# A hand-written instruction order, laid over the whole first layer and not over its first block alone

## The chip, the cores and the metric

The kernel runs on one core of a Trainium2 chip. The metric is device time in microseconds (us) of one execution. The kernel before has a median of 888.12 us over 3 runs (887.09 to 888.78).

The core has engines with an instruction queue each: TensorE (PE, matrix products; PEld is its loading of stationary operands), VectorE (DVE), ScalarE (ACT) and SyncE (SP), which here issues the DMAs. GpSimd (POOL) does four small instructions in this kernel. Each engine takes its instructions in the order in which they stand in the program for it, so the order is decided when the kernel is built, and an instruction whose operand is late holds up what stands behind it.

## The reference

```
# 1. attention: 4 x 8 heads, 576 positions, 64 wide; window 32, half the heads with every fourth key
scores = where(mask, scale * q @ k.T, -1e9); attn = softmax(scores); x = attn @ v      # -> 2304 x 512
# 2. layer 1: 2304 tokens, 512 -> 2048 -> 512, rational activation
h = x @ w_in;  P = a0 + a1 h + a2 h^2 + a3 h^3;  Q = 1 + |b0||h| + |b1|h^2
x = (P / (Q + 1e-6)) @ w_out
# 3. layer 2: the same sizes, PReLU
h = x @ w_in;  g = max(h, 0) + alpha * min(h, 0);  out = g @ w_out
```

## The kernel before, in words

**Precision.** A float32 operand is split in a high and a low part (`xh`, `xl`; `gh`, `gl`; `wouth`, `woutl`), and a product is three matmuls: high by high, low by high, high by low. To split costs one ACT copy and one DVE subtraction (L742, L743).

**Stages.** The tokens are six blocks of 384. Attention works in units of two heads and two segments, spread over the kernel's first 400 us or so and woven into layer 1. Layer 1 goes block by block; within a block over 16 chunks of 128 of the hidden width, two at a time, which gives 48 steps `J`. A step does the input product of its two chunks (`inproj`, L645, into the PSUM banks `ps_h`), the rational activation in two parts (`rat_1`: ACT L663, L664 and DVE L665, L666, which read `ps_h`, the last of them freeing the bank; `rat_2`: DVE L672, ACT L673 and L674, DVE L675 to L677), the split of the result (L684, L685: `gh`, `gl`) and, two steps later, the output product (`outproj1`, L695, groups of three matmuls). ACT and DVE also do the softmax of the attention unit that is due (L492 to L532), the making of the packed weights of both layers (L381 to L400, `win` and `wout` tiles) and the splitting of weights (L416, L417).

**Layer 2** works on double blocks (`n` is 0 to 2) and pairs of chunks (`q` is 0 to 7), so 24 calls of `st_pair`, `k` = 0 to 23. Each does seven products (`product`, L836) in place of eight, in the order p1 p6 p2 p7 p4 p5 p3, on sums and differences of the tokens (`st_B11`, `st_T1` to `st_T4`, `st_B21`, `st_B22`; made on DVE at L760 and split at L743) and of the weights (`st_s`, `st_a`; `st_prep`, L813 and L760, split at L743). The results are put together on DVE (L866) and ACT (L871), then PReLU (`st_prelu`, L843), its split (`st_g`), and the output product (`outproj2`, L714), which is queued in the list `todo` and taken from it by `out_some(k)`. What layer 1 has left in `todo` when layer 2 begins (16 groups of three matmuls) is taken between the products of pairs 0 and 1.

The tokens that layer 2 reads go through memory: layer 1 stores them (`y_dram<-os`), and `x_load` and `y_load` (L739) load them again, into buffers that attention's loads use before. So do the packed weights: `w_dram_in` is stored (L360) and later loaded (`w` at L806, L341).

**What sets the order.** The build puts instructions on each engine by their place in the code, as far as operands and buffers allow. The kernel lays an order of its own over this: `in_order_of_need` (L136) takes the instructions built, derives who needs whom from their regions, and gives each a duration (`_cost`) and a `level`, the length of the longest chain behind it. Then it plays the program through: at each step the engine that can start earliest takes, of what is ready, the instruction with the highest level. SP stays in the order of the code, and PE's matmuls are drawn to it. What starts before `ORDERED` (115e3 ns, in the list's own time) gets a dependency on its predecessor on the engine, without a semaphore; all that starts later is only placed behind the last of these, in the build's own order. For a DMA the list counts a transfer time, and then 900 ns until its data can be used, or 2700 ns when transfers queue.

**Places that the change and the steps touch.** L136 to L262 `in_order_of_need`; `st_pair` with its four `out_some(counts[..])`; the loop over `n` and `q` at the end of the kernel; L959 to L970 the matmuls on constant data that PE does at the start (`warm`, and `fill` on `msk`).

Of the kernel before, what the change touches and what calls it, by code (L numbers as in the profile page):

```python
# [29 lines left out]
FILLS = (64,)  # L30
W_BIAS = 2.0 ** -112
NARROW = 2.1
SLACK = 100.0
FILL = 256
ORDERED = 115e3
SIGNED = (('out', 4), ('out', 6), ('out', 8), ('out', 10), ('out', 12))
WARM = 10
ORDER = "cqiqpvqvqvvwwwwwwqvwwwwwwwwqv"
# [94 lines left out]
    return i.engine == mybir.EngineType.PE and _columns(i.outs[0]) == FILL  # L133


def in_order_of_need(tc, nc, places):  # L136


    Engine = mybir.EngineType
    todo = [  # L140
        i for i in nc.cur_bb.bb.instructions
        if i.engine in (Engine.PE, Engine.DVE, Engine.Activation, Engine.SP) and (i.ins or i.outs)
    ]
    n = len(todo)
# [80 lines left out]
            waiting[todo[k].engine].append(k)  # L225
    order = {e: [] for e in free}
    landed = 0.0
    for _ in range(n):
        pick = None
        for e, w in waiting.items():  # L230
            if not w:
                continue
            t = min(max(free[e], ready_at[k]) for k in w)
            if pick is None or t < pick[0]:
                pick = t, e
        t, e = pick
        limit = max(t, free[e]) + SLACK
        k = max((k for k in waiting[e] if ready_at[k] <= limit), key=lambda k: level[k])
        waiting[e].remove(k)
        start = max(free[e], ready_at[k])  # L240
        if start < ORDERED:
            order[e].append(k)
        free[e] = start + costs[k][0]
        if e == Engine.SP:
            parts, width = size[k]
            begin = max(start + 1600, landed)
            landed = begin + parts * width / (412 if parts == 128 else 210)
            done = landed + (2700 if begin > start + 1700 else 900)
        else:
            done = start + costs[k][1]  # L250
        for j, data in after[k]:
            left[j] -= 1
            ready_at[j] = max(ready_at[j], done if data else free[e])
            if not left[j]:
                waiting[todo[j].engine].append(j)
# [11 lines left out]
def attn_rational_prelu_kernel(  # L267
# [16 lines left out]
    nc = tc.nc  # L284
# [3 lines left out]
    slots = {}  # L288
# [563 lines left out]
    def st_pair(n, q, w, counts, before):  # L852

        c = 2 * q
        after = n + 1 if q == NQ - 1 and n + 1 < SB else 0

        def free(*names):
            for name in names if after else ():
                x_place(after, name)

        def fetch(name):
            if after:
                x_fetch(after, name)

        small = n == 0 and q < 2
        add = lambda out, a, b: nc.vector.tensor_tensor(out=out, in0=a, in1=b, op=ALU.add)  # L866
        p1 = product(n, w, "A11", "B11")
        p6 = product(n, w, "S2", "T2")
        v1 = ap_.tile([128, BLK], F32, tag="pts", name="v1", bufs=2)
        u2 = ap_.tile([128, BLK], F32, tag="p", name="u2")  # L870
        nc.scalar.activation(out=v1, in_=p1, func=AF.Copy)  # L871
        add(u2, v1, p6)
        if small:
            before()
        out_some(counts[0])
        fetch("B11")

        (h0, n0, g0), (h1, n1, g1) = (
            [tp.tile([128, 2 * BLK], F32, tag=f"t{s}", name=f"t{s}", bufs=2) for s in "abc"] for _ in range(2)
        )  # L880
        p2 = product(n, w, "A12", "B21")
        p7 = product(n, w, "S3", "T3")
        add(half(h0, 0), v1, p2)
        add(half(h1, 1), u2, p7)
        out_some(counts[1])
        fetch("B21")
        free("T2")

        p4 = product(n, w, "A22", "T4")
        p5 = product(n, w, "S1", "T1")  # L890
        add(half(h1, 0), half(h1, 1), p4)
        add(half(h1, 1), half(h1, 1), p5)
        add(u2, u2, p5)
        if small:
            st_prelu(c + 1, h1, n1, g1)
            out_some(counts[2])
        free("T3", "B11")

        p3 = product(n, w, "S4", "B22")
        add(half(h0, 1), u2, p3)  # L900
        if not small:
            before()
            free("B21", "T4", "T1", "B22")
            st_prelu(c + 1, h1, n1, g1)
        hl1 = st_g(g1)
        st_prelu(c, h0, n0, g0)
        out_some(counts[3])

        def rest():
            hl0 = st_g(g0)  # L910
            for i, hl in ((1, hl1), (0, hl0)):
                for b in range(2):
                    for t in range(3):
                        todo.append((
                            outproj2, (2, 2 * n + b, c + i), [half(x, b) for x in hl], t,
                            q == 0 and i == 1, q == NQ - 1 and i == 0,
                        ))
        return rest
# [175 lines left out]
    for n in range(SB):  # L1094
        for q in range(NQ):
            k = n * NQ + q

            def before():
                if rest:
# [17 lines left out]
                    if q == (6 if n == 0 else 5):  # L1117
                        x_combine(n + 1)

            rest = st_pair(n, q, st_ops.pop(k), ((4, 4, 3, 3), (2, 0, 0, 9), (0, 0, 0, 12))[min(k, 2)], before)  # L1120
    rest()
    out_some(len(todo))
    in_order_of_need(tc, nc, slots)


def _consts():
# [79 lines left out]
```

## Time and profile before

| | |
|---|---|
| median of 3 runs | 888.12 us (887.09 to 888.78) |
| the profiled execution | 887.51 us, of which the span 885.7 us |
| PE busy | 872.5 us (99%), 5746 matmuls |
| PEld busy | 779.0 us (88%) |
| DVE busy | 760.7 us (86%), 1199 instructions |
| ACT busy | 613.3 us (69%), 1253 instructions |
| moved by DMA | 92.78 MB, mean 105 GB/s |

The span is the time from the first recorded instruction to the last; some 1.8 us of the execution lie around it. Busy times are of the whole span; matmuls are pipelined, and two that overlap count as one stretch of busy time. PE busy for 99% therefore doesn't tell how fast matmuls followed each other; their starts do. In a stretch where nothing delays them, matmuls on 384 columns start 173 ns apart.

### The profile page before, as it was taken

The page shows a single profiled execution, that of the slowest core. Times are in us where ns is not written, and L with a number is a line of the kernel's source. Part 1 is how long each engine was busy: PE and PEld are TensorE (multiplying, and loading weights), DVE is VectorE, ACT ScalarE, POOL GpSimd, SP SyncE. Part 2 cuts the span into 40 slices and gives each one's busy share as a digit, 9 for nine tenths or more (in the row PEclk, how much of TensorE's full clock was granted, in tenths as well). Part 3 has the DMA queues.
Part 4 walks back from the last instruction along what each step waited for, and adds up shares of the span by engine and source line. Part 5 has one row for each costly group of instructions (what it writes and reads, how often), then busy time and mean ns, then how long its engine had stood idle before and what let it go on. Part 6 is the DMA issues. An engine that isn't in the chain of part 4 may idle for free.

```text
span 885.7 us, 14822 instructions
## 1 busy us (share of the span) xinstructions
PE 872.5 (99%) x5746; PEld 779.0 (88%) x5746; DVE 760.7 (86%) x1199; ACT 613.3 (69%) x1253; POOL 0.2 (0%) x4
## 2 busy tenths in 40 slices
PE   9999999999999999999999999999999999999997
PEld 6555678999999999999999999898888989899896
DVE  5999999999999998988899999998986778767652
ACT  6999988788877888887677576557554456635423
POOL 0000000000000000000000000000000000000000
PEclk9999999999999999999999999999999999999999
DMA  9964212133334434440021242323320011210001
GB/s 346 407 238 176 82 57 79 38 115 140 130 109 139 173 125 148 160 149 19 20 78 42 95 131 95 119 79 119 101 85 24 27 46 60 97 47 25 1 0 72
DMA packets 32903, 92.78 MB, mean 105 GB/s; under 512 B 3905, under 2 KB 11329, under 8 KB 32833
## 3 DMA queue, kind: packets, MB, share of 16 engines
q1 hardware_dynamic: 32832, 91.83, 29.9%
q8 instruction: 45, 0.74, 0.3%
q14 instruction: 26, 0.20, 0.1%
HBM read 76.61 MB, written 15.20 MB: 104 GB/s over the span
## 4 chain that ended last, share of the span: by engine, by line
PE 57%; ACT 18%; DVE 18%; DMA 4%; issue 2%; SPq 0%; ACTq 0%
PE ps_h L836 19%; PE ps_y L714 14%; PE ps_y L695 9%; PE ps_h L645 7%; PE ps_aS L714 4%; PE ps_aP L714 3%; ACT p L512 3%; DVE tb L675 2%; DVE tc L676 2%; ACT p L532 2%; ACT tc L664 2%; ACT ta L673 2%; DVE tc L677 2%; ACT ta L674 2%; ACT ta L663 1%
## 5 line engine op out<-in xcount | busy, mean ns | idle before, releaser
L645 PE MATMUL ps_h<-xh,winh 128*128 128x384 f32 x320 | 110.4, 345 | 2.7 <-DVE tc L666 2.2
L695 PE MATMUL ps_y<-gh,wouth 128*128 128x384 f32 x320 | 108.4, 339 | 0.0
L695 PE MATMUL ps_y<-gl,wouth 128*128 128x384 f32 x320 | 107.1, 335 | 0.3 <-DVE gl L685 0.3
L695 PE MATMUL ps_y<-gh,woutl 128*128 128x384 f32 x320 | 107.2, 335 | 0.0
L645 PE MATMUL ps_h<-xh,winl 128*128 128x384 f32 x320 | 107.2, 335 | 0.0
L645 PE MATMUL ps_h<-xl,winh 128*128 128x384 f32 x320 | 107.1, 335 | 0.0
L714 PE MATMUL ps_y<-wouth,gl 128*128 128x512 f32 x192 | 74.9, 390 | 0.0
L714 PE MATMUL ps_y<-woutl,gh 128*128 128x512 f32 x192 | 74.9, 390 | 0.0
L714 PE MATMUL ps_y<-wouth,gh 128*128 128x512 f32 x192 | 74.8, 390 | 0.0
L663 ACT ACTIVATE ta<-ps_h,root 128x384 f32<-128x384 f32 x96 | 57.3, 596 | 18.7 <-PE ps_h L645 18.4
L664 ACT ACTIVATE tc<-ps_h,co 128x384 f32<-128x384 f32 x96 | 66.5, 694 | 0.0
L645 PEld LDWEIGHTS ps_h<-xh,winh 128*128 128x128 f32 x320 | 60.0, 188 | 6.9 <-DVE tc L666 3.7
L742 ACT ACTIVATE gh<-tc 128x768 fp32r<-128x768 f32 x48 | 40.3, 841 | 30.5 <-PE ps_aP L714 28.0
L695 PEld LDWEIGHTS ps_y<-gl,wouth 128*128 128x128 f32 x320 | 60.2, 188 | 0.6 <-DVE gl L685 0.6
L645 PEld LDWEIGHTS ps_h<-xl,winh 128*128 128x128 f32 x320 | 60.1, 188 | 0.3
L743 DVE TENSOR_TENSOR gl<-tc,gh 128x768 fp32r<-128x768 f32 x48 | 45.8, 954 | 16.9 <-ACT gh L742 16.7
L695 PEld LDWEIGHTS ps_y<-gh,wouth 128*128 128x128 f32 x320 | 60.2, 188 | 0.0
L742 ACT ACTIVATE st_a<-w 128x1024 fp32r<-128x1024 f32 x24 | 25.5, 1061 | 50.1 <-PE ps_h L836 41.4
L695 PEld LDWEIGHTS ps_y<-gh,woutl 128*128 128x128 f32 x320 | 60.1, 188 | 0.0
L645 PEld LDWEIGHTS ps_h<-xh,winl 128*128 128x128 f32 x320 | 60.1, 188 | 0.0
L675 DVE SCALAR_TENSOR_TENSOR tb<-tb,ta 128x768 f32<-128x768 f32 x48 | 45.8, 955 | 16.3 <-ACT ta L674 16.0
L666 DVE SCALAR_TENSOR_TENSOR tc<-tc,co,ps_h 128x384 f32<-128x384 f32 x96 | 58.1, 608 | 0.7
(197 smaller groups left out, 2317.8 us busy)
## 6 DMA issues: line engine op xcount, KB each, us to landing
w<-w_dram_in SPq DMA_DIRECT2D x24, 512.0 KB, 3.6
raw<-in_w_in_dram SPq DMA_DIRECT2D x16, 512.0 KB, 5.1
raw_inh<-in_w_out_dram SPq DMA_DIRECT2D x13, 512.0 KB, 3.8
ld_qk<-in_qk_d_dram SPq DMA_DIRECT2D x12, 512.0 KB, 5.0
ld_v<-in_v_d_dram SPq DMA_DIRECT2D x12, 512.0 KB, 4.1
ld_qk<-in_qk_p_dram SPq DMA_DIRECT2D x12, 416.0 KB, 4.2
ld_v<-in_v_p_dram SPq DMA_DIRECT2D x12, 384.0 KB, 3.4
y_dram<-os SPq DMA_DIRECT2D x24, 192.0 KB, 1.9
```

Of the source, the lines that this page charges most:

```text
L512: nc.scalar.activation(out=a["p"][h][:m, t * n:(t + 1) * n], in_=a["s"][h][:m, t * n:(t + 1) * n], func=AF.Exp, scale=scale, bias=a["nm"][ ...
L532: nc.scalar.activation(out=pv, in_=pv, func=AF.Copy, scale=rd[:m, t:t + 1])
L645: nc.tensor.matmul(out=hp[:, :BLK], lhsT=w, rhs=x, start=(k == 0), stop=(k == len(pairs) - 1))
L663: nc.scalar.activation(out=ta, in_=hp, func=AF.Abs, scale=root)
L664: nc.scalar.activation(out=tc_, in_=hp, func=AF.Identity, scale=co[:, 3:4], bias=co[:, 2:3])
L666: nc.vector.scalar_tensor_tensor(out=tc_, in0=tc_, scalar=co[:, 1:2], in1=hp, op0=ALU.add, op1=ALU.mult)
L675: nc.vector.scalar_tensor_tensor(out=tb, in0=tb, scalar=C1, in1=ta, op0=ALU.add, op1=ALU.mult)
L695: nc.tensor.matmul(out=yt[:, :BLK], lhsT=w[:, m * 128:(m + 1) * 128], rhs=g, start=(c == 0 and i == 0), stop=(c == NC - 1 and i == len(pai ...
L714: nc.tensor.matmul(out=yt, lhsT=g[:, tok], rhs=w, start=(first and i == 0), stop=(last and i == 2))
L742: nc.scalar.activation(out=hi, in_=t, func=AF.Copy)
L743: nc.vector.tensor_tensor(out=lo, in0=t, in1=hi.bitcast(F32), op=ALU.subtract)
L836: nc.tensor.matmul(out=hp, lhsT=u[:, ws], rhs=x[:, xs], start=(k == 0), stop=(k == 5))
```

## The change

1. `in_order_of_need` is given only the instructions that are built before pair `k = LISTED = 1` of layer 2, that is attention, all of layer 1 and pair 0 of layer 2 without the part called `rest`. `ORDERED` goes from 115e3 to 2000e3 ns, so all of these get an order. What is built later gets none from the list.
2. The delay between a transfer's end and its use: it was 2700 ns where transfers queue and 900 ns elsewhere. It is now `min(2700, 300 + 450 * transfers issued before)` for the first twelve and wherever they queue, so 300 ns for the first, 750 for the second, and 2700 from the seventh on.
3. The 16 groups left from layer 1 are all taken in pair 0 of layer 2, four at each of its four places (before 4, 4, 3 and 3, and two in pair 1). `out_some(counts[3])` moves ahead of the last PReLU and its split, and pairs from 1 on take 12 groups there (pair 1 took 9 before, and 2 at its first place).

```
-ORDERED = 115e3
+LAG = 2700
+LISTED = 1
+ORDERED = 2000e3
...
-def in_order_of_need(tc, nc, places):
+def in_order_of_need(tc, instructions, places):
...
-        i for i in nc.cur_bb.bb.instructions
+        i for i in instructions
...
     landed = 0.0
+    issued = []
...
-            done = landed + (2700 if begin > start + 1700 else 900)
+            done = landed + (min(LAG, 300 + 450 * len(issued)) if begin > start + 1700 or len(issued) < 12 else 900)
+            issued.append(k)
...
         if not small:
             before()
             free("B21", "T4", "T1", "B22")
+            out_some(counts[3])
             st_prelu(c + 1, h1, n1, g1)
+        else:
+            out_some(counts[3])
         hl1 = st_g(g1)
         st_prelu(c, h0, n0, g0)
-        out_some(counts[3])
...
             k = n * NQ + q
+            if k == LISTED:
+                listed = len(nc.cur_bb.bb.instructions)
...
-            rest = st_pair(n, q, st_ops.pop(k), ((4, 4, 3, 3), (2, 0, 0, 9), (0, 0, 0, 12))[min(k, 2)], before)
+            rest = st_pair(n, q, st_ops.pop(k), ((4, 4, 4, 4), (0, 0, 0, 12), (0, 0, 0, 12))[min(k, 2)], before)
     rest()
     out_some(len(todo))
-    in_order_of_need(tc, nc, slots)
+    in_order_of_need(tc, nc.cur_bb.bb.instructions[:listed], slots)
```

In the changed kernel the lines of the code in question have numbers that are higher by 4. The names below have the number of their tile behind them.

**Place 1: DVE at the start of the second block of layer 1** (around 230 to 236 us in the trace of before). `tc_2662` and `tb_2661` belong to the block's first step, `sm_2691` and `rd_2708` to the softmax of the attention unit that is due, `gl_2811` to the step before the last. Before:

```order
L685 TENSOR_TENSOR gl_2811<-tc_2512,gh_2810 128x768
L396 SCALAR_TENSOR_TENSOR win2_2983<-raw_2981,win2_2983 128x512
L522 TENSOR_SCALAR sm_2691<-sm_2691 112x8
L523 RECIPROCAL rd_2708<-sm_2691 112x8
L665 TENSOR_TENSOR tc_2662<-tc_2662,ps_h_2663 128x384
L672 SCALAR_TENSOR_TENSOR tb_2661<-ta_2660,ratio_112 128x768
L666 SCALAR_TENSOR_TENSOR tc_2662<-tc_2662,co_110,ps_h_2663 128x384
```

And after:

```order
L669 TENSOR_TENSOR tc_2662<-tc_2662,ps_h_2663 128x384
L500 TENSOR_SCALAR nm_2642<-mx_2641 112x8
L670 SCALAR_TENSOR_TENSOR tc_2662<-tc_2662,co_110,ps_h_2663 128x384
L689 TENSOR_TENSOR gl_2811<-tc_2512,gh_2810 128x768
L676 SCALAR_TENSOR_TENSOR tb_2661<-ta_2660,ratio_112 128x768
L669 TENSOR_TENSOR tc_2662<-tc_2662,ps_h_2676 128x384
L670 SCALAR_TENSOR_TENSOR tc_2662<-tc_2662,co_110,ps_h_2676 128x384
L526 TENSOR_SCALAR sm_2691<-sm_2691 112x8
L527 RECIPROCAL rd_2708<-sm_2691 112x8
```

The two readers of the bank `ps_h_2663` (L669 and L670) stand ahead of `gl_2811`, of the softmax sums and of L676; before they stood behind all of these. On ACT the instruction that they need (L664 before, L668 after) stood behind the eight exponentials of `sm_2691`, and now stands ahead of all eight.

**Place 2: DVE at the end of layer 1** (around 482 to 500 us in the trace of before). `tc_5494`, `tc_5573` and `tc_5667` are the activations of the last three steps of layer 1. Before:

```order
L676 SCALAR_TENSOR_TENSOR tc_5494<-tc_5494,co_110,ta_5492 128x768
L665 TENSOR_TENSOR tc_5573<-tc_5573,ps_h_5574 128x384
L677 SCALAR_TENSOR_TENSOR tc_5494<-tb_5493,tc_5494 128x768
L666 SCALAR_TENSOR_TENSOR tc_5573<-tc_5573,co_110,ps_h_5574 128x384
L665 TENSOR_TENSOR tc_5573<-tc_5573,ps_h_5587 128x384
L672 SCALAR_TENSOR_TENSOR tb_5572<-ta_5571,ratio_112 128x768
L666 SCALAR_TENSOR_TENSOR tc_5573<-tc_5573,co_110,ps_h_5587 128x384
L685 TENSOR_TENSOR gl_5709<-tc_5494,gh_5708 128x768
```

And after:

```order
L680 SCALAR_TENSOR_TENSOR tc_5494<-tc_5494,co_110,ta_5492 128x768
L764 TENSOR_TENSOR st_T1_5397<-st_T3_5396,st_B11l_5393 128x768
L681 SCALAR_TENSOR_TENSOR tc_5494<-tb_5493,tc_5494 128x768
L669 TENSOR_TENSOR tc_5573<-tc_5573,ps_h_5574 128x384
L764 TENSOR_TENSOR st_T3_5396<-st_B22_5399,st_T3_5396 128x768
L670 SCALAR_TENSOR_TENSOR tc_5573<-tc_5573,co_110,ps_h_5574 128x384
L764 TENSOR_TENSOR st_t2_5479<-st_B22_5399,st_T1_5397 128x768
L669 TENSOR_TENSOR tc_5573<-tc_5573,ps_h_5587 128x384
L676 SCALAR_TENSOR_TENSOR tb_5572<-ta_5571,ratio_112 128x768
L670 SCALAR_TENSOR_TENSOR tc_5573<-tc_5573,co_110,ps_h_5587 128x384
L764 TENSOR_TENSOR st_T4_5398<-st_B21l_5395,st_t2_5479 128x768
L689 TENSOR_TENSOR gl_5709<-tc_5494,gh_5708 128x768
```

`st_T1_5397` is the first of the instructions with which DVE prepares layer 2's first pair. Of these, 16 stood ahead of the first row of this piece before, and all 16 stand behind it now, woven into the rows up to p1's successor on DVE (`u2_5767`) and a few behind that.

**Place 3: SP, the loads for layer 2.** `w_dram_in14` is the store of the last packed weight tile of layer 2, `st_...` the loads of its tokens. Before:

```order
L441 DMA ld_v_4535<-in_v_d_dram 128x1024
L739 DMA st_T3_5396<-y_dram1_0_88 128x384
L739 DMA st_T3_5396<-y_dram1_1_89 128x384
L341 DMA w32_5488<-w_dram_out0_2658 128x1024
L360 DMA w_dram_in14_5244<-win14_5236 128x1024
L806 DMA w32_5490<-w_dram_in0_2278 128x1024
L739 DMA st_B11l_5393<-y_dram0_0_84 128x384
```

And after:

```order
L706 DMA y_dram4_3_103<-os_5229 128x384
L360 DMA raw_5232<-in_w2_in_dram 128x1024
L360 DMA raw_5234<-in_w2_in_dram 128x1024
L364 DMA w_dram_in14_5244<-win14_5236 128x1024
L743 DMA st_B11l_5393<-y_dram0_0_84 128x384
L743 DMA st_B11l_5393<-y_dram0_1_85 128x384
L743 DMA st_T3_5396<-y_dram1_0_88 128x384
L743 DMA st_T3_5396<-y_dram1_1_89 128x384
```

The token loads stand behind the store of `win14`, whose making on DVE ends, after the change, one row behind L680 of `tc_5410`, the step before `tc_5494`. Before, `win14` was made and stored some 90 us earlier in the trace, and only the first token load stood ahead of it.

## Rows read from the trace of the kernel before

**Rows 1.** The page: busy time of each engine, and the chain that ended last.

```profile
PE 872.5 (99%) x5746; PEld 779.0 (88%) x5746; DVE 760.7 (86%) x1199; ACT 613.3 (69%) x1253; POOL 0.2 (0%) x4
...
PE 57%; ACT 18%; DVE 18%; DMA 4%; issue 2%; SPq 0%; ACTq 0%
```

**Rows 2.** Windows: busy us and instructions by engine, clock, DMA share, GB/s.

```profile
4.40:20.00 15.60, 15.52 (x266) 12.29 (x266) 9.46 (x33) 10.57 (x62) 0.00 (x0) 1.00 1.01 392
20.00:120.00 100.00, 96.78 (x638) 60.14 (x635) 97.72 (x168) 98.92 (x227) 0.00 (x0) 1.00 0.56 210
120.00:440.00 320.00, 316.62 (x2591) 301.80 (x2590) 296.59 (x462) 257.80 (x638) 0.00 (x0) 1.00 0.33 110
440.00:484.00 44.00, 44.00 (x256) 44.00 (x255) 42.91 (x59) 31.57 (x47) 0.00 (x0) 1.00 0.16 52
484.00:520.00 36.00, 36.00 (x206) 35.56 (x205) 34.61 (x51) 23.63 (x36) 0.00 (x0) 1.00 0.32 101
520.00:640.00 120.00, 119.30 (x598) 107.33 (x597) 114.28 (x178) 72.94 (x95) 0.00 (x0) 1.00 0.31 103
```

**Rows 3.** Waits of PE from 120 to 440 us: us in total, times, longest.

```profile
PE ps_h L645 <- DVE tc L666: 2.2, 4, 0.8
PE ps_h L645 <- DVE xl L615: 0.5, 1, 0.5
PE ps_h L582 <- ACT wouth L416: 0.4, 1, 0.4
PE ps_y L695 <- DVE gl L685: 0.3, 1, 0.3
```

**Rows 4.** Timeline of PE, one such wait: start, us, [idle <- releaser].

```profile
234.19 0.34 PE L695 MATMUL ps_y<-gh,woutl 128*128 128x384 f32 x1
235.28 0.45 PE L645 MATMUL ps_h<-xh,winh 128*128 128x384 f32 x1 [0.75 <-DVE tc L666]
```

**Rows 5.** Timeline of PE at the start, alike matmuls together.

```profile
2.14 3.00 PE L963 MATMUL ps_h<-warm 128*128 128x512 bf16 x8
...
6.11 2.58 PE L967 MATMUL ps_h<-msk 128*128 128x256 bf16 x22
8.62 0.29 PE L478 MATMUL ps_aS<-ld_qk 64*64 64x96 f32 x1
```

**Rows 6.** Timeline of ACT ahead of 233 us: first and last exponentials.

```profile
230.02 0.33 ACT L512 ACTIVATE p<-ps_aS,nm 112x80 f32<-112x80 f32 x1 [0.16 <-DVE nm L496]
...
232.37 0.24 ACT L512 ACTIVATION_READ_ACCUMULATOR p<-ps_aP,nm 112x1 f32 x1
232.47 0.71 ACT L664 ACTIVATE tc<-ps_h,co 128x384 f32<-128x384 f32 x1
```

**Rows 7.** Timeline of DVE, there and at 476 and 483 us.

```profile
233.21 0.55 DVE L665 TENSOR_TENSOR tc<-tc,ps_h 128x384 f32<-128x384 f32 x1 [0.15 <-ACT tc L664]
233.68 1.02 DVE L672 SCALAR_TENSOR_TENSOR tb<-ta,ratio 128x768 f32<-128x768 f32 x1
234.61 0.61 DVE L666 SCALAR_TENSOR_TENSOR tc<-tc,co,ps_h 128x384 f32<-128x384 f32 x1
...
476.12 1.01 DVE L676 SCALAR_TENSOR_TENSOR tc<-tc,co,ta 128x768 f32<-128x768 f32 x1
...
483.44 1.01 DVE L676 SCALAR_TENSOR_TENSOR tc<-tc,co,ta 128x768 f32<-128x768 f32 x1
```

**Rows 8.** Lines of DVE from 400 to 484 us: xcount, busy us, mean ns, idle.

```profile
L417 DVE TENSOR_TENSOR woutl<-w,wouth 128x1024 fp32r<-128x1024 f32 x1 | 1.2, 1218 | 0.0
L743 DVE TENSOR_TENSOR st_a<-w,st_a 128x1024 fp32r<-128x1024 f32 x1 | 1.2, 1217 | 0.0
...
L760 DVE TENSOR_TENSOR st_T<-st_T,st_B11l 128x768 f32<-128x768 f32 x1 | 0.9, 945 | 0.0
...
L760 DVE TENSOR_TENSOR st_s<-w,st_s 128x256 f32<-128x256 f32 x1 | 0.4, 415 | 0.0
```

**Rows 9.** Timeline of PE: first matmul of p1, of p4, of pair 1's p1.

```profile
498.00 0.33 PE L836 MATMUL ps_h<-st_B11h,st_a 128*128 128x384 f32 x1
...
506.32 0.33 PE L836 MATMUL ps_h<-st_T4h,st_a 128*128 128x384 f32 x1
...
512.56 0.33 PE L836 MATMUL ps_h<-st_B11h,st_a 128*128 128x384 f32 x1
```

**Rows 10.** Timeline of SP's queue from 383 to 403 us.

```profile
383.07 0.79 SPq L739 DMA_DIRECT2D st_T<-y_dram  x2
...
389.13 0.49 SPq L360 DMA_DIRECT2D w_dram_in<-win  x1
...
402.82 0.80 SPq L739 DMA_DIRECT2D st_B<-y_dram  x2
```

**Rows 11.** DMA issues from 380 to 405 us: KB each, us to landing.

```profile
w<-w_dram_in SPq DMA_DIRECT2D x1, 512.0 KB, 5.5
st_T<-y_dram SPq DMA_DIRECT2D x2, 192.0 KB, 3.2
...
st_B<-y_dram SPq DMA_DIRECT2D x2, 192.0 KB, 3.5
```

## The prediction

> **What bounds the kernel now.** I read the page's busy line and the chain first [rows 1], then the windows by stage, which say more. From 20 to 120 us ACT and DVE are busy for 98.92 and 97.72 of 100 us and PE's loads for only 60.14: attention and the making of weights bound that stage. From 120 us on it is PE: 316.62 of 320 us to 440, then all of 44, all of 36, and 119.30 of 120 [rows 2]. But DVE stands close behind: 42.91 of 44, 34.61 of 36, 114.28 of 120. So from 120 us there are two questions only: how much of PE's idle time goes, and whether DVE, which has 1.1 us to spare from 440 to 484 and 1.4 us from 484 to 520, can take work that comes later than it did.
>
> The waits of PE from 120 to 440 us add up to 2.2 + 0.5 + 0.4 + 0.3 = 3.4 us in seven places [rows 3]. One of the four on DVE's L666, of up to 0.8 us, shows in the timeline [rows 4]: the last matmul of the old block starts at 234.19, the first of the new at 235.28, where one step is 0.17; the interval lost is therefore 0.92 us, and 0.75 of it is idle.
>
> **The first 115 us.** The list ordered these before too. What changes in them comes from the smaller landing delays and the other levels. Along DVE and ACT the same instructions change places by one or two; the work ahead of any of them moves by about 1 us and back, and nothing leaves this stage. PE gets three of its ten warm matmuls and ten of its 22 fillers (the 22 take 2.58 us [rows 5]) moved behind products of attention; these products begin when their data lands (8.62 us in rows 5), so the fillers were no work that anything waited for. I take 0, with 1.5 us to either side: the moved fillers and warm matmuls take 10 x 2.58 / 22 + 3 x 3.00 / 8 = 2.3 us [rows 5], and more than half of that would have to fall on the path.
>
> By the Trainium skill, "TensorE: Matmul & The Clock Gate", section "Part 1: The HAM clock gate", TensorE's clock comes up with activity and falls without it, so fillers taken away could leave the first products at 1.2 GHz; the rows show a granted clock of 1.00, which is 2.4 GHz, from 4.4 us on [rows 2], with the fillers in place, and cannot show the other case. It would cost at most the start's own products twice, inside the 1.5 us.
>
> **Layer 1 from 120 to 440 us: the gain.** Why PE waited at 235: ACT does eight exponentials from 230.02 on, and reaches L664 at 232.47 [rows 6]; then DVE does L665, L672 (1.02 us) and L666, which frees the bank at 234.61 + 0.61 = 235.22 [rows 7]; PE goes on at 235.28. After the change (place 1) L664's successor stands ahead of all eight exponentials, 2.4 us sooner, and DVE has both readers of the bank ahead of the step's 1.02 us. Either alone covers 0.92 us. The same pattern stands at the starts of the next blocks, with alike moves: that is L666's 2.2 us. The other three waits (0.5, 0.4, 0.3) are single ones, each with its releaser further ahead after the change. The gain is 3.4 us by idle time; by the starts of the matmuls it is 4.7 us over the seven, as 0.92 stands for 0.75 at 235 us, since each new start adds some 0.2 us. I take 4.0. It can't be more than 4.7: elsewhere in the stage PE waits for nothing. It is less where the list, which knows costs only, makes waits of its own; so 2 to 4.7.
>
> **The end of layer 1: the loss.** DVE's preparation for layer 2's first pair stood spread between 406 and 482 us, ahead of L676 of `tc_5494` (483.44 us [rows 7]). In the changed order sixteen of these instructions stand behind that row (place 2). They are ten on 768 columns, of which one stands in rows 8 (0.95 us each), two on 1024 (1.22 each) and four on 256 (0.42 each) [rows 8]: 10 x 0.95 + 2 x 1.22 + 4 x 0.42 = 13.6 us. On DVE an instruction follows the one before some 0.08 us before that one's recorded end (233.68 + 1.02 to 234.61 in rows 7), so they occupy 12.3 us. What would they have instead? Ahead of 484 DVE has 12 us less to do and nothing to do it for: PE is full from 440 to 484 [rows 2], so layer 1's steps come no sooner, and DVE just waits. Behind 484 it has 34.61 + 12.3 = 46.9 us of work in a stretch of 36. Some other preparation (two splits of 768 and part of pair 1's) moves still further behind, which leaves 11.6 us ahead of the first PReLU of pair 0.
>
> How much of that reaches PE? Following both engines down the new order, from 484 on, with durations from these rows: each DVE instruction starts when the one before it is through and its operands are there, and each product starts when its bank is free and its split tokens and weights are there.
> - p1 needs the low part of `st_a`: it comes 2.3 us later than 498.00 [rows 9].
> - p6 needs the bank that the last L670 of layer 1 frees, behind twelve of the sixteen: 4.1 us late. p2 and p7 follow at about 4.
> - p4 (506.32 [rows 9]) needs a bank that DVE's L870 frees behind the split of T4: 6.1; p5 and p3 6.2 and 6.4.
> - p1 of pair 1 (512.56 [rows 9]): 6.8; its p6 and p7 7.1 and 7.6; the first output products, which need `gl` of pair 0, 7.6.
>
> The delay grows while DVE's backlog of 11.6 us lasts, less the slack that each product had against its bank or `gl` (by the trace's starts and ends 0.3 to 4 us). From about 530 us on DVE, with 120 - 114.28 = 5.7 us to spare up to 640 [rows 2], falls behind no further, and PE has the delay and keeps it, because it has no idle time to give back. I take 8 us, from 6 (the slacks larger than I count, or the output products of layer 1, now sixteen groups in this pair, filling part of the wait) to 10 (the tail of the backlog delays pair 1's products once more).
>
> **Loads.** `win14` is made later now, and the token loads stand behind its store on SP (place 3). In the trace of before they were issued at 383 to 403 us [rows 10]; now not before DVE is through with the last row of `win14`, right behind L680 of `tc_5410`; that step is 7 us ahead of `tc_5494` (476.12 against 483.44 in rows 7), so about 477.5 us. The first four loads, which `st_T1` needs, go out by 479.5 at 0.4 us each [rows 10] and land 3.2 to 3.5 us later [rows 11], at 483, when DVE comes to it; behind it on DVE stand the activations of layer 1's last two steps, for which PE would have to wait. I take 0, with 4 us more if loads land later.
>
> **Layer 2 behind that and the end.** PE's two waits at 623 to 625 us (the rest of 120 - 119.30 [rows 2]) may go or stay: 0, to 0.7 either way. All of layer 1's output groups in pair 0, and 12 in place of 9 + 2 in pair 1, move PE work earlier and shorten the list of output products left at the end by three groups; their matmuls are done all the same, so the sum is 0.
>
> **Sum.** 887.5 - 4.0 + 8 + 0 = 891.5 us against the profiled execution of 887.51, whose span of 885.7 has 1.8 us around it. It lies 0.6 us below the median of 888.12, which I let stand: forecast 891.5, 3.4 us above the median. A difference under 0.2% (1.8 us) can't be told from no change here.
>
> **Rivals.**
> - *Only PE's gaps count.* The waits of layer 1 go and the preparation, though late, finds DVE free: DVE gets ahead before 484 after all, or the list put it as late as it is needed and no later. Then 887.5 - 4.0 + 0 to 1.5 = 883.5 to 885. For it: the list knows how long DVE is busy, and puts the chain of layer 2 by its length. Against it: 46.9 us do not fit in 36. Chance 0.22. This is what the Trainium skill, "Perfetto Trace Analysis", section "Optimization Strategy", would have one do: find the gaps on the engine that bounds the stage and what it waits for. It doesn't count the second engine, which has no gaps there either [rows 2].
> - *Both cancel.* The delay of p1 to p4 is half of what I work out, because sixteen groups of layer 1 (48 x 0.173 = 8.3 us of matmuls) cover it: 887.5 - 4 + 4 = 887.5. Chance 0.2.
> - *Loads late, one place more.* The store of `win14` holds the loads on SP, 8 token loads and then three loads of 512 KB land after DVE asks for them, and DVE stands at `st_T1` in front of layer 1's last two activations: on top of 891.5 come the 3.2 to 5.5 us that such a load takes [rows 11], so 894.7 to 897. For it: SP now is in the order of the code up to there. It decides if the store is issued after 480 us. Chance 0.13.
> - *The change does nothing beyond 115 us*, the order being held by operands: 888. The two orders differ at places 1 to 3, and the waits at 235 come from order alone, so 0.03.
> - The forecast: 0.42.
>
> **How the numbers follow.** Forecast and late loads are slower by over 0.2% (above 889.9) but for the forecast's lowest end: 0.42 + 0.13 = 0.55. The first rival is faster (below 886.3), 0.22, and a bit of the second, 0.03: 0.25. The rest, 0.2, is no change. The range is to leave out 2 in 10: from 884.0, which leaves out the lower part of the first rival (some 0.1), to 896.5, above which the upper part of the third lies, and loads that are later still. The forecast's own range is 889 to 894.5.
>
> **What would show it.** Right: PE's waits for L670 between 120 and 440 us gone; DVE idle for some 10 us between 440 and 484 and then without a gap to about 530; p1 at about 498 - 4 + 2.3, p4 4 + 2 us later against it than before, the waits of PE in 490 to 520 on DVE lines L670, L870 and L747. Wrong: PE without gaps from 484 to 520 (first rival); DVE waiting at `st_T1` for a DMA (third); a stage before 120 us that changed its length by more than 1.5 us, of which I have no term.

## The result, and the profile after

The changed kernel takes 893.03 us (median of 7 runs, 892.0 to 895.8), the kernel before in the runs beside it 887.78. The ratio is 1.0065, with a 95% interval of 1.005 to 1.0079: it is slower, by 4.4 to 7.0 us. The profiled execution took 892.0 us, with a span of 890.2 us, 4.5 us more than that of before.

The page of the changed kernel, the lines that answer to [rows 1]:

```profile
PE 874.9 (98%) x5745; PEld 778.6 (87%) x5746; DVE 758.2 (85%) x1199; ACT 615.1 (69%) x1253; POOL 0.2 (0%) x4
...
PE 79%; DVE 9%; ACT 8%; issue 2%; DMA 1%; SPq 0%; ACTq 0%; DVEq 0%
```

Its windows, as in [rows 2]:

```profile
20.00:120.00 100.00, 96.35 (x645) 59.73 (x643) 96.46 (x166) 97.59 (x227) 0.00 (x0) 1.00 0.53 200
120.00:440.00 320.00, 319.40 (x2615) 305.95 (x2615) 287.85 (x451) 255.17 (x636) 0.00 (x0) 1.00 0.29 99
440.00:484.00 44.00, 43.43 (x251) 43.11 (x250) 41.08 (x58) 29.37 (x46) 0.00 (x0) 1.00 0.31 108
484.00:520.00 36.00, 32.47 (x174) 29.40 (x172) 36.00 (x52) 23.30 (x32) 0.00 (x0) 1.00 0.33 110
520.00:640.00 120.00, 119.35 (x595) 106.70 (x595) 115.27 (x179) 72.94 (x98) 0.00 (x0) 1.00 0.33 111
```

Two of these rows hold the two terms of the prediction. From 120 to 440 us PE now idles 0.6 us, where it was 3.4. From 484 to 520 DVE is busy without a break, 36.00 of 36, and PE, which was full there, loses 3.5 us of busy time and does 174 matmuls in place of 206. The waits of PE, first from 120 to 440 us (compare [rows 3]), then from 440 to 540, where the kernel before has none:

```profile
PE ps_h L649 <- DVE xl L619: 0.3, 1, 0.3
```

```profile
PE ps_h L840 <- DVE ta L870: 1.8, 1, 1.8
PE ps_y L699 <- ACT gh L688: 0.8, 1, 0.8
PE ps_h L840 <- ACT v L875: 0.7, 1, 0.7
PE ps_y L699 <- ACT os L705: 0.6, 1, 0.6
PE ps_h L840 <- DVE st_a L747: 0.5, 1, 0.5
PE ps_h L840 <- DVE u L870: 0.3, 1, 0.3
PE ps_y L699 <- DVE gl L689: 0.2, 1, 0.2
```

DVE's timeline of the changed kernel, where the preparation begins and where the first wait behind it stands (in between no gap is longer than 0.14 us):

```profile
480.37 0.96 DVE L679 SCALAR_TENSOR_TENSOR tb<-tb,ta 128x768 f32<-128x768 f32 x1 [1.43 <-ACT ta L678]
481.25 1.01 DVE L680 SCALAR_TENSOR_TENSOR tc<-tc,co,ta 128x768 f32<-128x768 f32 x1
482.18 0.95 DVE L764 TENSOR_TENSOR st_T<-st_T,st_B11l 128x768 f32<-128x768 f32 x1
...
523.54 0.43 DVE L817 TENSOR_TENSOR st_s<-w 128x256 f32<-128x256 f32 x1 [0.16 <-DMA w<-w_dram_in]
```

SP's queue of the changed kernel, in answer to [rows 10]:

```profile
445.38 0.33 SPq L364 DMA_DIRECT2D w_dram_in<-win  x1
445.75 6.43 SPq L706 DMA_DIRECT2D y_dram<-os  x4
452.29 0.90 SPq L360 DMA_DIRECT2D raw<-in_w_in_dram  x2
474.15 0.33 SPq L364 DMA_DIRECT2D w_dram_in<-win  x1
476.78 0.80 SPq L743 DMA_DIRECT2D st_B11l<-y_dram  x2
```

And two of SP's waits between 440 and 490 us (us in total, times, longest); the longest of the first stands ahead of the row at 474.15, the second ahead of the last row:

```profile
SPq L364 <- DVE win L400: 31.7, 2, 21.0
SPq L743 <- DMA w_dram_in<-win: 2.2, 1, 2.2
```

The row at 452.29 shows what the prediction did not follow to its root: the raw weights for `win14` are loaded only behind block 4's four stores. SP then stands 21.0 us at the store of `win14`, until DVE has packed it between layer 1's steps (its last row ends at 474.12). The token loads come behind that store, at 476.78. They were issued from 383 us on before.

To see where time goes I line the traces up by work left: for each trace, the time at which a given amount of the matmul work of the two layers is still to be done (0.1733 us for a matmul on 384 columns, 0.227 on 512; some 750 us in all). The table gives the time in the kernel before, and how much later each other kernel reaches the same point. All work counts alike, so the differences hardly depend on the order of the groups.

| work left, us | 705 | 435 | 400 | 355 | 260 | 250 | 10 |
|---|---|---|---|---|---|---|---|
| before reaches it at | 118.54 | 442.01 | 477.02 | 522.10 | 617.82 | 629.26 | 870.82 |
| changed | +1.45 | -2.60 | -1.73 | +5.34 | +5.88 | +4.64 | +4.51 |
| e1, loads early in the code | +3.97 | +8.44 | +14.31 | +14.40 | +14.63 | +14.04 | +14.33 |
| e2, LISTED = 3 | +4.49 | +0.31 | +1.18 | +7.86 | +9.73 | +8.35 | +8.61 |
| e3, old delays | +0.48 | -3.39 | -2.52 | +4.84 | +5.44 | +4.08 | +4.06 |
| e4, 7 warm matmuls | +3.61 | -0.48 | +0.38 | +8.19 | +10.34 | +9.00 | +9.43 |
| e5, SP free | +3.03 | -2.25 | -2.25 | -2.17 | -1.92 | -3.18 | -1.13 |
| e6, packing early | +4.76 | +10.13 | +10.13 | +12.87 | +13.41 | +12.31 | +12.32 |
| e7, old counts | +4.77 | +0.58 | +1.45 | +9.35 | +9.77 | +8.50 | +8.44 |
| e8, before with the new counts | +2.34 | +2.07 | +2.07 | +2.20 | +2.19 | +0.95 | +0.99 |
| e9, ordered to 115 us | +2.04 | +4.41 | +4.41 | +4.58 | +4.59 | +4.49 | +4.20 |
| e10, SP free, old delays | +1.06 | -3.49 | -3.49 | -3.41 | -2.23 | -3.49 | -2.70 |

The changed kernel's row reads: +1.45 by the end of attention's dense part, a gain of 4.05 over layer 1, a loss of 0.87 in one place between 442 and 477, a loss of 7.07 between 477 and 522 and 0.54 more behind it, and 1.24 given back where the kernel before waits at 623 us.

Each row is one execution, and in most of them TensorE's granted clock falls from 1.00 to 0.50 (2.4 to 1.2 GHz) for some microseconds. In the traces of before, of the changed kernel and of e3 it doesn't fall before the end. In e8, e9 and e10 it is at 0.50 for 3.4 us from 35 or 37 us on; in e2, e4, e6 and e7 for 6.8 us from 33 to 35 us on; in e1 for 3.4 us from 37 us on, in e5 for 3.4 us from 82 us on. Later falls: e1 at 382 us (10.2 us) and 467 us (3.4), e6 at 305 us (10.2), e7 at 503 us (3.4). The first column is therefore no measure of a kernel's order alone; the steps from column to column are, where no fall lies between.

### The profile page after: what moved, and what is told of

Read it like the earlier page. It is cut to its first block, busy times and chain, and to the rows that moved or that the text cites. A ratio compares the mean times of both kernels' runs of the same rounds, so it can differ in the third digit from the quotient of the medians.

```text
span 890.2 us, 14823 instructions
## 1 busy us (share of the span) xinstructions
PE 874.9 (98%) x5745; PEld 778.6 (87%) x5746; DVE 758.2 (85%) x1199; ACT 615.1 (69%) x1253; POOL 0.2 (0%) x4
## 4 chain that ended last, share of the span: by engine, by line
PE 79%; DVE 9%; ACT 8%; issue 2%; DMA 1%; SPq 0%; ACTq 0%; DVEq 0%
PE ps_h L840 19%; PE ps_h L649 16%; PE ps_y L699 16%; PE ps_y L718 15%; PE ps_aS L718 4%; PE ps_aP L718 4%; PE ps_h L586 2%; ACT p L516 1%; DVE tb L679 1%; DVE tc L680 1%; ACT win L379 1%; DVE tc L669 1%; DVE tc L681 1%; ACT tc L668 1%; PE ps_aS L553 1%
## 5 line engine op out<-in xcount | busy, mean ns | idle before, releaser
L668 ACT ACTIVATE tc<-ps_h,co 128x384 f32<-128x384 f32 x96 | 66.2, 690 | 0.0
L677 ACT ACTIVATE ta<-tb,c1t 128x768 f32<-128x768 f32 x48 | 46.4, 967 | 20.0 <-DVE tb L676 20.0
```

The source lines that it names most:

```text
L668: nc.scalar.activation(out=tc_, in_=hp, func=AF.Identity, scale=co[:, 3:4], bias=co[:, 2:3])
L677: nc.scalar.activation(out=ta, in_=tb, func=AF.Ln, bias=c1t)
```

## The experiments

All are edits of the changed kernel, except e8. All compute the whole result. The ratios are against the kernel before in runs beside them, whose medians were 887.88 us (e1 to e4), 888.56 (e5 to e8) and 888.3 (e9, e10).

**e1, the loads early in the code.**

```
-        if J >= NC and early and (J - NC) * 5 // 13 > (J - NC - 1) * 5 // 13:
+        if J >= NC and early and (J - NC) * 7 // 13 > (J - NC - 1) * 7 // 13:
...
-        if J == NP - 5:
+        if J == NP - 9:
             x_load(0)
```

> The changed kernel with two places of its code moved, so that on SP the raw loads of the last packed weights and the token loads of layer 2 stand ahead of the stores of block 4 and not behind them; the list is as it was. Theory A (the preparation bunches up on DVE because SP in code order brings its tokens late): the list puts st_T1 some 40 us sooner, DVE has no 40 us without a gap from 481 on, PE's idle time from 440 to 540 falls from 4.9 us to under 1.5, the loss of 7 to 8 us goes, and the time is 884 to 886.5 us, below the kernel before (887.8) and the changed one (893.0). Rival B (the levels, not the data, put the preparation last): no change, 892 to 894. Rival C (DVE simply has too much to do in the last 80 us of layer 1): part of the loss stays, 888 to 891.

Measured: 901.49 us, ratio 1.015 (1.0132 to 1.0168). The time missed by 15 us, and the stage in question did what theory A says: from 484 to 530 PE is full, and the table's row is flat from 400 to 355 (14.31 to 14.40).

```profile
484.00:530.00 46.00, 46.00 (x268) 46.00 (x267) 45.39 (x66) 30.03 (x44) 0.00 (x0) 1.00 0.27 90
```

What was lost lies elsewhere. At 381 us PE has waited 2.0 us for ACT (L572), and at 386 us another 3.0 for DVE (L670), and from 382 us on the clock is at 0.50 for 10.2 us; the window (PE busy, granted clock, DMA share, GB/s):

```profile
381.00:393.00 12.00, 8.38 (x79) 0.57 0.24 93
```

At the second place it is SP's queue again. SP and ACT of this kernel at 442 to 465 us:

```profile
442.88 0.80 SPq L743 DMA_DIRECT2D st_T<-y_dram  x2
460.87 0.79 SPq L743 DMA_DIRECT2D st_B21l<-y_dram  x2
461.71 5.02 SPq L706 DMA_DIRECT2D y_dram<-os  x4
```

```profile
464.48 0.49 ACT L705 ACTIVATE os<-ps_y 128x384 f32<-128x384 f32 x1 [6.75 <-DMA y_dram<-os]
```

Nothing is issued for 17 us: at the head stand token loads that wait for their buffer. Block 4's stores stand behind them, ACT waits 6.75 us for an output buffer, and PE for ACT (3.8 us). My edit cleared one thing out of SP's way and put another in.

**e2, a list that sees further** (`LISTED = 3`).

> The changed kernel with LISTED = 3 in place of 1, so the list sees two more pairs of layer 2 and the chains behind the preparation are longer. Theory A (data late on SP): the loss from 480 to 530 us stays, since win14's raw loads and the token loads are issued as before; 893 us, within 1.5. Rival B (the list's horizon ends too soon, so the preparation has too low a level): the preparation comes sooner, under 889 us.

Measured: 895.15 us, ratio 1.008 (1.0061 to 1.0099). From 400 to 355 left it loses 6.68 us, as the changed kernel does (7.07). A horizon three pairs wide doesn't remove the loss; rival B falls. In its profile the rest above 893 is the start, where ACT, DVE and SP have the changed kernel's order over the first 120 us, but the clock is at 0.50 from 34.6 us on for 6.8 us.

**e3, the old landing delays.** `(min(LAG, ...) ... else 900)` becomes `(LAG if begin > start + 1700 else 900)`.

> The changed kernel with the landing delays of the kernel before (2700 or 900 ns). At the start the order is the same on PE and DVE as in the changed kernel; some rows change places behind 480 us. Theory: the delays have no part in the start's loss of 1.4 us nor in the gain of layer 1; 893 us, within 1.5. Rival (the smaller delays cost the start 1.4 us, as the prediction had them as one of two causes): 891.6.

Measured: 892.02 us, ratio 1.0053 (1.0035 to 1.0071). The loss at the end of layer 1 stays (7.36 us from 400 to 355), and so does the gain (3.87 from 705 to 435). Its start is 0.48 us later than before, at 10 us as at 118; the changed kernel's is 1.45 later. Whether that is the delays isn't shown: below, one and the same start differs by as much from execution to execution.

**e4, three warm matmuls less** (`WARM = 7`).

> The changed kernel with 7 warm matmuls on constant data in place of 10: the three that stand behind the masks, ahead of and behind attention's first products, are gone. They are no part of the result. Theory: these three are the start's +0.95 us, since the first product of attention starts at 6.17 us behind them and at 5.36 in the kernel before; it starts at about 5.4 again, and the time is 892.1, 0.6 to 1.2 below the changed kernel. Rival (the products wait for data anyhow): 893.0, no change. Rival (the clock comes up later with less work on PE): the granted clock of the first windows falls below 1.00 and the time rises to 894 or more.

Measured: 895.47 us, ratio 1.0077 (1.0058 to 1.0095): not faster, and the first product of attention starts at 6.06 us, no sooner than the changed kernel's 6.17 to speak of. The edit didn't free that time: the list put three fillers in the place of two of the matmuls taken out (`msk`, from 5.30 us on, 0.82 us), so the theory on the warm matmuls stays untested. The rival on the clock doesn't have it either in its own words: the clock comes up at 6.12 us here and at 6.00 in the changed kernel. What is new in this profile comes later. Windows of PE (busy, granted clock, DMA share, GB/s):

```profile
32.00:34.00 2.00, 0.85 (x4) 0.86 1.01 402
34.00:36.00 2.00, 2.00 (x14) 0.50 1.04 407
36.00:38.00 2.00, 2.00 (x26) 0.50 1.03 410
38.00:40.00 2.00, 2.00 (x4) 0.50 1.02 409
40.00:42.00 2.00, 2.00 (x22) 0.94 1.03 412
```

For about 7 us the clock is at 0.50, the lower of its two levels, behind a stretch in which PE stood waiting for attention's softmax on ACT and was busy for only 0.85 of 2 us. The profiled execution of the changed kernel has the same wait:

```profile
33.16 0.84 PE L553 MATMUL ps_aS<-ident,p 128*96 128x128 f32 x3 [1.89 <-ACT p L536]
```

and a clock of 1.00 behind it. That the missing warm matmuls make the difference isn't shown: e2 and e7 have all ten, the same wait and the same fall, and e4's two runs at a mean clock of 0.997 and 0.998 (892.4 and 893.4 us) lie where the changed kernel's lie at 0.997 and 0.998 (892.7 to 895.7).

**e5, SP free in the list.**

```
-    fixed = {Engine.PE: None, Engine.SP: None}
+    fixed = {Engine.PE: None}
```

> The changed kernel, but the list no longer keeps SP in the order of the code (one word taken out of a dictionary); SP's instructions take their place by readiness and level as those of DVE and ACT do. Its SP order then is nearly that of the kernel before from the loads for the last packed weights on: the token loads stand ahead of block 4's stores. Theory A (SP in code order is what makes the preparation late): the loss from 480 to 530 us goes (PE idle there under 1 us), the gain of layer 1 stays, and the time is 883.5 to 886, below the kernel before at 887.9. It differs from the first experiment in that no token load of the next double block stands in SP's queue ahead of block 4's stores without its buffer being free. Rival B (SP's order can't be changed without a new wait elsewhere, as in the first experiment with 6.7 us of ACT on its output buffers): 888 or more.

Measured: 885.88 us, ratio 0.9974 (0.9958 to 0.999): faster than the kernel before, and 7 us below the changed one, within the range of theory A. Its first token loads are issued at 396.72 us (`st_B11l`), the first preparation runs on DVE at 404.97 and not at 482:

```profile
396.72 0.79 SPq L743 DMA_DIRECT2D st_B11l<-y_dram  x2
404.97 0.95 DVE L764 TENSOR_TENSOR st_T<-st_T,st_B11l 128x768 f32<-128x768 f32 x1
```

The end of layer 1 in its windows:

```profile
440.00:484.00 44.00, 44.00 (x256) 44.00 (x255) 42.15 (x59) 31.76 (x49) 0.00 (x0) 1.00 0.15 49
484.00:530.00 46.00, 46.00 (x255) 44.48 (x254) 44.58 (x68) 30.81 (x45) 0.00 (x0) 1.00 0.36 121
```

PE is full again, its waits from 440 to 560 us are none, and the table's row from 400 to 355 moves by 0.08 where the changed kernel's moves by 7.07. Layer 1's gain stays: 5.28 from 705 to 435. The edit frees SP throughout and so changes the order of the start too; that it is the loads of `win14` and of the tokens which matter at the end of layer 1 rests on e1 and e6 beside it, which move only the packing with its loads and, in e1, the token loads. Behind 250 left it gives 2 us back, with two waits of PE for ACT's L875 (1.8 us).

**e6, only the packing earlier** (factor 6 in place of 5, token loads where they were).

> The changed kernel with the packing of late weights a little sooner in the code (factor 6 in place of 5), so that win14 is packed before block 4's stores; the token loads stay where they were in the code, behind these stores. SP then issues the token loads at about 452 us in place of 477. Theory A: the preparation starts some 25 us sooner and about half of it is over by 484; 888 to 890.5. Rival B (levels): 892 to 894.

Measured: 899.34 us, ratio 1.0118 (1.0092 to 1.0145), a miss of 10 us. Of the loss at the end of layer 1 some 2.7 are left (10.13 to 12.87), as theory A has it or better. But the list now took the packing as urgent at another place. DVE at 302 us, and the windows behind it:

```profile
302.48 0.69 DVE L385 TENSOR_SCALAR win<-win 128x1024 uint32<-128x1024 uint32 x1 [2.56 <-ACT win L379]
```

```profile
302.00:306.00 4.00, 2.10 (x35) 1.68 (x36) 3.48 (x6) 3.96 (x8) 0.00 (x0) 0.86 0.02 4
306.00:310.00 4.00, 1.11 (x25) 0.87 (x20) 4.00 (x7) 0.84 (x1) 0.00 (x0) 0.50 0.59 229
```

DVE waits 2.56 us for ACT's part of the packing, with an activation that PE needs queued behind; PE waits 1.8 and 2.9 us, and its clock falls to 0.50 for 10.2 us, as in e1.

**e7, the old counts**, and **e8, the new counts alone in the kernel before.**

> The changed kernel with the counts of output groups, and their place ahead of the last PReLU, as before. Theory: the counts have no part in the loss at 484 to 530, and give the 1.2 us by which layer 2 behind 530 us is faster; 894, between 893 and 895. Rival (the sixteen groups in pair 0 are what PE does while it waits for DVE, so without them the loss is larger): 895 to 897.

> The kernel before with only the counts and the place of the output groups changed. Theory: PE's waits at 623 us go and three groups less are left at the end; 886.7 to 887.5 against 887.9. Rival (worth nothing): 887.9, within 0.4.

Measured: e7 893.27 us, ratio 1.0066 (1.0043 to 1.0089); e8 888.2 us, ratio 0.9996 (0.9983 to 1.0009). The counts are worth nothing that the runs can tell. In the profile of e8 the kernel is 1.24 us quicker past 623 us, where PE's two waits are gone, as in the changed kernel. But e7, which has the old counts, gains 1.27 us there (260 to 250 left), and e9, which has the new ones, only 0.10, with a wait of 0.9 us at that place. So the counts alone don't decide these waits, and what does stays open. In e7 the loss at the end of layer 1 is 7.9 us, 0.8 more; its clock falls within that stretch (window as above), so this says nothing for the rival:

```profile
502.00:507.00 5.00, 4.65 (x16) 0.66 0.25 93
```

**e9, the order to 115 us only** (`ORDERED = 115e3`).

> The changed kernel with ORDERED = 115e3 as before: the list is played through as in the changed kernel, but only its first 115 us become an order. DVE's rows at the end of layer 1 and SP's loads stand as in the kernel before. Theory: neither the gain of layer 1 (4 to 5 us) nor the loss from 450 to 530 us (8 us) is there, the waits of PE for L670 at the block starts are back; what is left is the start's loss of 0.5 to 1.5 us and the 1.1 us that the counts spare at 623 us: within 1 us of the kernel before. Rival (the loss comes from the counts or from another part, and not from what is ordered behind 115 us): 2 us or more above the kernel before.

Measured: 891.44 us, ratio 1.0047 (1.003 to 1.0064). Half right: the row is flat from 435 to 260, so the loss at layer 1's end belongs to what is ordered behind 115 us. But it is 3 us slower than I expected. It loses 2.04 us up to 705, with a fall of the clock at 35 us in it, and then 2.4 more up to 435, with waits of 4.3 us in the middle of layer 1 where the kernel before has 3.4. Why the rest, in the build's own order, comes out worse behind another first part isn't shown. The rival's threshold of 2 us was passed for another reason than the one it names.

**e10, SP free, with the old landing delays.**

> The kernel of the fifth experiment (SP free in the list) with the landing delays of the kernel before. Alone, the old delays took 0.5 us off the start. Theory (the start is helped by the older, longer delays in either order): gain of layer 1 and no loss at its end as in the fifth experiment, the start 0.5 to 1.5 us better, 884 to 885.5. Rival (with SP free, the delays decide which load goes first, and the old ones bring attention's late): 886 or more.

Measured: 884.74 us, ratio 0.9959 (0.9945 to 0.9972), the lowest median of all: 3.6 us below the kernel before, 8 below the changed one, and within the theory's range. The intervals of e5 and e10 overlap, and the two profiles have their falls of the clock at different places (82 and 35 us), so that the old delays help the start isn't shown.

## Why the prediction was right, and where it was not

The forecast was 891.5; the profiled execution took 892.0 and the median is 893.03. By steps:

- **Layer 1's gain.** Predicted 4.0, from 2 to 4.7; measured 4.05 between 705 and 435. PE's waits for L670 at the block starts are gone from the list, and in e9, without the order behind 115 us, they are back (2.2 and 0.7 us) and the gain isn't there. Right in cause and size; which of the two moves of place 1 does it was not tested apart.
- **The end of layer 1.** Predicted 8, from 6 to 10; measured 7.07 + 0.54. The sixteen instructions do run behind L680 of `tc_5494` (482.18 against 481.25), and DVE stays busy from 481 to 523. The cause is shown: e5, e1 and in the main e6 bring the token loads sooner and take the loss away, e2, e3 and e7 leave them late and keep it. The way through the single products is less right than the sum. First matmuls of p1, p6, p4 and of pair 1's p1 in the changed kernel (compare [rows 9]):

```profile
496.40 0.41 PE L840 MATMUL ps_h<-st_B11h,st_a 128*128 128x384 f32 x1
499.57 0.44 PE L840 MATMUL ps_h<-st_T2h,st_s 128*128 128x384 f32 x1
509.30 0.44 PE L840 MATMUL ps_h<-st_T4h,st_a 128*128 128x384 f32 x1 [1.80 <-DVE ta L870]
517.49 0.41 PE L840 MATMUL ps_h<-st_B11h,st_a 128*128 128x384 f32 x1 [0.31 <-DVE u L870]
```

  Delays against the -1.73 that each would have had: p7 3.9 (predicted 4), p3 7.2 (6.4), p1 of pair 1 6.7 (6.8); but p1 0.1 at its first matmul and 0.9 at its last (2.3), p6 2.3 (4.1), p2 2.6 (4), p4 4.7 (6.1), p5 4.3 (6.2). I counted these five too late by 1.4 to 2.2 us each, and one of them for a wrong reason: p6 starts at 499.57, before the last L670 of layer 1 ends (499.51 + 0.60), so the bank that I named doesn't hold it. No wait for L670 is in the list. What stands ahead of p6 is a wait of 0.8 us for `gh` (ACT's L688), which itself waits for DVE's L681.
- **What DVE does before 484.** Wrong. I had it idle for some 10 us between 440 and 484; it is busy for 41.08 of 44, as the packing of `win14` and others have moved in. The idle time lies further ahead: 287.85 us from 120 to 440, where it was 296.59. The sum did not rest on that.
- **Token loads.** Predicted at 477.5, without a wait at `st_T1`; issued at 476.78, and `st_T1` starts without a gap. Right. I named the store of `win14` as what holds them, which is so (SP's waits of 21.0 and 2.2 us). That the raw loads of `win14` in turn stand behind block 4's stores I had not seen; with these loads moved ahead, 2.7 us of the loss are left (e6).
- **Not foreseen.** 0.87 us at 451, where the list puts the third and fourth copy of block 4's output behind six activations on ACT, at 450.87 (PE's 0.6 us for L705). Before, each of the four copies had one activation between it and the next.
- **Start.** Predicted 0, with 1.5 either way; measured +1.45 in the profile. The bound held; whether the value did can't be told from single profiles. In e8 ACT, DVE and SP have the order of the kernel before over the first 120 us, and still it is 0.86 us later at 10 us and 2.34 at 118. The clock comes up at 4.38 us in the trace of before and at 6.24 in e8's, and the same ten matmuls take (before, then e8):

```profile
1.32 3.83 PE L963 MATMUL ps_h<-warm 128*128 128x512 bf16 x10 [1.32 <-DVE c1t L981]
1.31 4.45 PE L965 MATMUL ps_h<-warm 128*128 128x512 bf16 x10 [1.31 <-DVE c1t L983]
```

  The prediction had attention's next products (8.62 us in [rows 5]) begin when their data lands; in e8 they begin at 9.48, as before at the end of the 22 fillers, so they do wait for these. In the changed kernel's profile the clock comes up at 6.00 us. Four profiles have the changed kernel's order there (its own, e2, e7 and e9); at 20 us, before any fall, they are between 0.41 and 1.83 us late, the changed kernel 1.29. A difference of +1.45 isn't clear of that.
- **Behind 530 us.** Predicted 0, 0.7 either way; measured -1.24, outside that: PE's waits at 623 us and the refilling behind them. The counts don't explain it (e7).

So 1.45 - 4.05 + 0.87 + 7.07 + 0.54 - 1.24 - 0.13 = 4.51, where the prediction had 4.0. That it comes so near is in part luck: the start's 1.45 and the 1.24 behind 530 us, both put at 0, nearly cancel. The two terms that the prediction rested on came out at 4.05 and 7.6.

The median is 0.7 us above that sum, and there the clock comes in. Of the changed kernel's seven runs one had a mean granted clock of 1.0 (892.0 us), the others 0.996 to 0.998 (892.7 to 895.8). Of the 51 runs of the kernel before beside the experiments 26 had 0.999 or 1.0; the sixteen at 1.0 took 886.0 to 888.7. The prediction held the cost of a low clock at the start to be inside 1.5 us and had no term for a later fall. Reckoned as in the table, but with attention's products counted too, e8 goes from 0.86 us behind the kernel before (at 30 us) to 2.39 (at 60 us): 1.5 us for a fall of 3.4 us. Against the changed kernel, which has the same order there, e2 and e7 lose 2.7 and 3.1 us by falls of 6.8 us. By the Trainium skill, "TensorE: Matmul & The Clock Gate", section "Part 1: The HAM clock gate", the clock is low by default and activity lifts it. The rows of e4 agree in so far as the fall stands behind PE's wait; they don't tell why the changed kernel stays at 1.00 behind the same wait.

Of the rivals, "only PE's gaps count" failed at DVE's 36.00 of 36. "Both cancel" had the layer 1 groups cover half of the delay; PE fell behind by 7.07 us with the sixteen groups in pair 0, and by 7.9 without them (e7, with a fall of the clock in it), so they covered little. "Loads late" did not come at `st_T1`, but SP's code order, which it named as its reason, is the root of the main loss.

What stays open: whether the order of the first 30 us costs anything, what decides PE's waits at 623 us, and why the clock falls in some executions and not in others. A list without the cut at `LISTED` but ordered to the end was not run.

## What to carry to other kernels

A list schedule that keeps one queue in program order inherits the waits of that queue: look in the trace for what stands at its head, since here a load held behind an unrelated store came back as a burst of work on another engine. When work is moved later on an engine that is 95% busy, add up its busy time behind the new place; here the overflow went to the engine that waits for it, less the slack of the first few consumers. To prove such a cause, free the queue: moving single loads by hand (e1, e6) removed the loss or most of it and made others. And before a single profile's start is put down to an edit, compare it with a second execution of the same order, and read the granted clock of both.

## What the runs showed of the hardware that I had not expected

The granted clock falls to 0.50 for 3.4 or 6.8 us in some executions and not in others, with the same order of the same instructions on ACT, DVE and SP. Behind a wait of PE of 1.9 us at 33 us it stays at 1.00 in the changed kernel's profile and falls in those of e2, e7 and e9; behind waits of 0.9 and 0.6 us it stays at 1.00 in before's and falls in e8's. PE in the changed kernel, in e2, in before and in e8:

```profile
37.00:42.00 5.00, 5.00 (x39) 1.00 1.03 411
37.00:42.00 5.00, 5.00 (x24) 0.56 1.02 408
37.00:42.00 5.00, 5.00 (x38) 1.00 1.04 412
37.00:42.00 5.00, 5.00 (x32) 0.66 1.02 408
```

By the sums above such a fall costs 1.5 to 3.1 us of 890, up to three quarters of what the new order gains in layer 1. And the time at which the clock first comes up differs by 1.9 us between two executions with one order (before at 4.38, e8 at 6.24 us), and e8 is 0.86 us late at 10 us.
